# The first head pair's q and k loaded and turned in row halves, with a newly laid out instruction order

## The chip, the cores and the metric

The kernel runs on one NeuronCore of a Trainium2 chip. The metric is the device time of one execution in microseconds (us), here given as the median of several runs. The engines named below are TensorE (PE; its weight loads are listed as PEld), VectorE (DVE), ScalarE (ACT), GpSimd (POOL) and SyncE (SP), which here only issues DMAs.

## The reference

Two layers follow each other. The first is attention with a mixture of blocks: for each of 4 batches x 8 heads, a sequence of 768 positions with head dimension 64 is cut into 12 key blocks of 64. Each query scores the mean key of every block that is not later than its own, keeps the best three and its own block, and attends causally inside those:

```
k_rep = k.reshape(B, H, 12, 64, D).mean(axis=3)
gate  = einsum('bhsd,bhnd->bhsn', q, k_rep)          # later blocks: -1e9
sel   = top3(gate) | {own block};  mask = sel & causal
attn  = softmax(where(mask, q @ k.T / 8, -1e9)) @ v
```

The second takes the heads side by side as x (4 x 768 x 512), mixes it by a two-dimensional Fourier transform, normalizes and applies a two-layer MLP:

```
u   = x + real(fft2(x))                 # over sequence and features
un  = (u - mean) / sqrt(var + 1e-6)
out = u + relu(un @ w1) @ w2            # 512 -> 2048 -> 512
```

## The kernel before, in words

Heads are taken in 16 pairs P (two heads, 128 partitions); four pairs make a batch b. Every step of the kernel is a short token such as `tk:3` (step and pair) or `w:0,5` (step, batch, tile). The text `ORDER` lists all tokens, and each engine executes its instructions strictly in that order. `PLACES` says which buffer each tile gets. Nothing is reordered later, so an engine that waits holds all of its own later instructions.

Steps for a pair P:

- `Lk`, `Lq`, `Lv` (`load`, lines 284 to 309): DMAs issued by SP that bring k, q and v. The first pair's q and k are loaded by `consts_first` (line 755) instead, one k half by ACT's queue.
- `tk`, `tq` (`a_tp`): k and q are turned so that the head dimension lies on partitions. For P of 2 to 6 that is TensorE's transpose, six tiles of 128x128 a tensor (line 350). For the pairs in `R3` it is a matmul with an identity matrix per head and row triple (line 338, 12 instructions a tensor, which the profile lists as 24). From P = 7 on DVE does it (line 325).
- `ks`, `kh` (lines 353 to 366): DVE sums the keys of each block, and the sums are spread over the two heads of the pair (`half`, on POOL).
- `kc`, `qc`, `qs`: k copied to 16 bit by ACT, q copied out of PSUM by DVE (for P = 0 half by ACT, half by DVE), q cast by POOL.
- `g`, `gt`, `gx`, `gl`, `gm`: PE computes the gate scores, DVE turns them, finds the best three, compares and turns the mask back.
- `K` (P of 7 and more): POOL copies the mask into extra rows of q, eight copies of 32x160 (`stage_K`).
- `s`, `e`, `d`: six score tiles a pair on PE, their exponentials on ACT (line 507), the causal cut on the diagonal on POOL (line 513).
- `vc`, `v`, `x`: v cast on POOL, product with v on PE, division on DVE.

Steps for a batch b: `fs`, `fd`, `f`, `fc` fold x for the Fourier transform (DVE, a little POOL); `y`, `ty`, `tr`, `m`, `u`, `nm`, `xu`, `xt`, `un` do the transform and the normalization's mean (PE, ACT, DVE in turn); `w`, `r` are the first MLP product and its ReLU (16 tiles); `bn`, `nv`, `nr` the variance; `c`, `o`, `od` the second MLP product, the sum and the output. `W` and `X` are POOL-issued loads of the MLP's weights.

`iz` spreads a small constant (`indc`, loaded by ACT's queue) over two tiles on ACT; the masks of pairs 0 to 6 need it. Before any of this PE runs nine matmuls of zeros (`warmps`, line 772) while the first loads are on their way.

Of the kernel before, what the change touches and what calls it, by code (L numbers as in the profile page):

```python
# [11 lines left out]
FP = mybir.dt.float32  # L12
# [79 lines left out]
for _pieces in SC_TILES:  # L92
# [16 lines left out]
R3 = (0, 1)  # L109
# [20 lines left out]
d:4,1 d:4,2 d:4,0 d:5,0 Lv:4 d:4,5 vc:4 v:4 xu:0,5 xt:0,4 xt:0,5 un:0,2 nm:0,1,1 xu:0,1 nm:0,2,1  # L130
xt:0,0 xt:0,1 un:0,0 x:4 nm:0,3,1 w:0,5,2 w:0,6,2 xu:0,3 w:0,5,0 xu:0,2 xt:0,2 xt:0,3 w:0,6,0
w:0,4,2 w:0,4,0 un:0,1 w:0,5,1 Lk:7 tk:7 gx:6 gl:6,0 ks:7 gl:6,1 gm:6 d:5,3 qs:7 W:2 kh:7 d:5,1
# [3 lines left out]
w:0,13 r:0,13 Lq:8 tq:8 Lc:0 K:7 s:7,5 e:7,5 s:7,2 e:7,2 w:0,15 r:0,15 d:6,3 d:6,4 d:6,1 d:6,5 kh:8  # L136
s:7,4 g:8 gt:8 gx:8 d:7,5 qs:8 X:0 Lv:6 vc:6 Lk:9 tk:9 gl:8,0 ks:9 Lq:9 tq:9 gl:8,1 fs:5,0 fs:5,1
gm:8 e:7,4 d:7,4 s:7,1 e:7,1 s:7,0 e:7,0 d:7,0 d:7,2 d:6,2 w:0,1 r:0,1 w:0,9 w:0,10 r:0,10 r:0,9
kc:8 bn:0,0 v:6 s:7,3 w:0,12 r:0,12 x:6 bn:0,4 bn:0,3 fs:6,0 fs:4,1 w:0,8 r:0,8 e:7,3 w:0,11 r:0,11
kh:9 X:1 qs:9 K:8 s:8,3 e:8,3 fs:4,0 g:9 gt:9 s:8,1 s:8,0 s:8,4 e:8,0 e:8,1 gx:9 gl:9,0 fs:6,1  # L140
gl:9,1 gm:9 d:7,1 Lv:7 vc:7 d:7,3 v:7 x:7 fd:6,1 fd:6,0 fs:7,1 fs:7,0 fd:7,0 bn:0,2 c:0,0,0 c:0,2,0
c:0,1,0 K:9 d:8,3 kc:9 e:8,4 Li:0 s:9,1 e:9,1 s:9,0 e:9,0 c:0,3,0 fd:7,1 fc:1 f:1,0 f:1,2 f:1,1 nv:0
nr:0 s:9,5 e:9,5 f:1,3 y:1,1,0 y:1,1,1 ty:1,1 tr:1,1 Lv:9 Lk:10 tk:10 ks:10 y:1,0,0 y:1,0,1 ty:1,0
tr:1,0 Lk:11 tk:11 ks:11 s:9,4 e:9,4 c:0,3,1 c:0,2,1 s:8,2 o:0,3 Lq:10 o:0,2 tq:10 Lk:12 m:1,2 u:1,5
e:8,2 kc:10 od:0,3 od:0,2 Lq:11 Lq:12 Lv:8 c:0,1,1 kh:10 g:10 d:8,2 d:9,5 gt:10 gx:10 u:1,4 m:1,0
u:1,0 s:9,3 e:9,3 c:0,0,1 s:8,5 e:8,5 d:9,0 kh:11 vc:9 u:1,1 tk:12 gl:10,0 m:1,1 u:1,3 u:1,2 o:0,1
gl:10,1 gm:10 tq:11 o:0,0 ks:12 nm:1,4,2 nm:1,0,2 xu:1,5 xu:1,4 un:1,4 s:9,2 e:9,2 nm:1,2,2 xu:1,1
un:1,1 c:0,4,0 c:0,4,1 o:0,4 kc:11 xu:1,3 un:1,3 xu:1,0 un:1,0 d:8,0 d:9,4 d:9,3 qs:10 d:8,1 d:9,1
d:9,2 v:9 g:11 K:10 s:10,4 e:10,4 gt:11 x:9 gx:11 gl:11,0 gl:11,1 tq:12 gm:11 c:0,5,0 xu:1,2 un:1,2
s:10,0 s:10,3 s:10,2 e:10,3 e:10,2 bn:1,5 c:0,5,1 o:0,5 bn:1,1 e:10,0 s:10,1 e:10,1 qs:11 d:8,5  # L150
d:8,4 vc:8 v:8 s:10,5 e:10,5 x:8 K:11 s:11,4 e:11,4 fs:9,0 d:10,4 s:11,2 kh:12 g:12 gt:12 e:11,2
s:11,0 s:11,1 e:11,0 e:11,1 s:11,3 e:11,3 d:11,4 d:11,1 d:10,3 d:10,1 d:11,3 d:10,0 un:1,5 w:1,11
r:1,11 fs:9,1 w:1,3 r:1,3 Lk:13 tk:13 gx:12 gl:12,0 gl:12,1 Lv:11 Lq:13 gm:12 K:12 w:1,15 s:11,5
e:11,5 d:11,0 w:1,0 w:1,14 r:1,14 kc:12 w:1,10 bn:1,2 r:1,15 ks:13 kh:13 d:11,5 d:11,2 vc:11 r:1,0
Lk:14 od:0,4 Lv:10 r:1,10 w:1,2 w:1,9 r:1,9 bn:1,4 d:10,5 qs:12 w:1,13 tq:13 r:1,2 Lv:14 bn:1,0 g:13
r:1,13 d:10,2 v:11 vc:10 bn:1,3 Lv:12 nv:1 s:12,5 w:1,12 od:0,5 e:12,5 gt:13 gx:13 Lk:15 w:1,7
r:1,12 x:11 kc:13 w:1,6 gl:13,0 r:1,7 od:0,1 fs:8,0 s:12,4 gl:13,1 Lq:14 gm:13 s:12,3 e:12,4 fs:8,1
v:10 K:13 tk:14 e:12,3 w:1,1 x:10 kc:14 qs:13 w:1,5 tk:15 Lq:15 r:1,1 w:1,4 r:1,5 fs:11,0 ks:15 nr:1
r:1,6 s:13,1 ks:14 od:0,0 s:13,5 w:1,8 e:13,5 r:1,4 fs:10,0 tq:14 s:12,2 r:1,8 fs:11,1 c:1,0,0
fd:11,1 e:13,1 tq:15 kh:15 kh:14 s:13,3 fs:10,1 s:12,1 fd:10,1 c:1,1,0 fd:11,0 e:12,1 fd:10,0 fc:2  # L160
e:13,3 f:2,1 f:2,2 s:13,0 e:12,2 f:2,3 c:1,0,1 f:2,0 e:13,0 d:12,2 d:13,3 s:12,0 d:12,3 g:15 e:12,0
d:12,5 g:14 d:13,1 c:1,1,1 gt:14 vc:14 gx:14 Lv:15 y:2,0,0 o:1,1 y:2,1,0 o:1,0 y:2,1,1 od:1,1
y:2,0,1 ty:2,1 c:1,4,0 vc:15 ty:2,0 tr:2,1 Lv:13 tr:2,0 od:1,0 m:2,1 d:12,1 d:12,0 d:13,0 m:2,0
u:2,3 u:2,2 c:1,4,1 u:2,0 nm:2,2,2 u:2,1 m:2,2 gl:14,0 nm:2,0,2 gl:14,1 xu:2,2 gm:14 bn:2,2 xu:2,3
c:1,5,0 K:14 gt:15 gx:15 c:1,2,0 o:1,4 vc:12 u:2,4 od:1,4 un:2,3 qs:14 gl:15,0 u:2,5 c:1,3,0 bn:2,3
nm:2,4,2 xu:2,5 un:2,2 bn:2,0 xu:2,1 d:13,5 s:13,4 qs:15 c:1,3,1 e:13,4 un:2,1 gl:15,1 bn:2,5 xu:2,4
un:2,5 s:13,2 gm:15 xu:2,0 c:1,2,1 e:13,2 un:2,0 kc:15 d:13,2 d:13,4 s:14,0 un:2,4 o:1,3 d:12,4
# [34 lines left out]
def kernel(  # L202
# [113 lines left out]
    def XW(P):  # L316
        return 1 if P in (0, 1, 2, 6) else 0
# [548 lines left out]
```

## Time and profile before

| | |
|---|---|
| median of 3 runs | 284.73 us (284.0 to 284.99) |
| profiled execution | 284.95 us |
| its span, first to last instruction | 283.3 us |
| busy: PE, DVE, ACT, POOL | 276.4, 188.7, 167.6, 122.3 us |
| granted TensorE clock | 1.00 in the whole span |

The span is what the profiler saw between the first and the last instruction; the 1.65 us to the execution's own time lie outside of it. Busy times of PE are unions of matmul records whose ends are modelled, so a busy PE isn't always a PE at full rate.

### The profile page before, as it was taken

To read this page: it belongs to the slowest core of one execution; us is meant where nothing else is said; L and a number is where in the kernel's file an instruction comes from. 1 tells how busy PE (TensorE), PEld (TensorE's weight loads), DVE (VectorE), ACT (ScalarE), POOL (GpSimd) and SP (SyncE) were. 2 spreads that over 40 slices of the span, in tenths; PEclk is the share of its full clock that TensorE was granted. 3 is DMA by queue.
4 is the path that set the end of the run, shared out by engine and by line. 5 is a ranking of instruction groups with operands and counts; after the bars stand their busy time and mean duration, and the time that the engine had idled before them with its cause. 6 is when DMAs were issued, how large, how long until landed. Compare 5 with 4: busy or idle time off the path is not lost.

```text
span 283.3 us, 6782 instructions
## 1 busy us (share of the span) xinstructions
PE 276.4 (98%) x2629; PEld 172.7 (61%) x2629; DVE 188.7 (67%) x568; ACT 167.6 (59%) x221; POOL 122.3 (43%) x314
## 2 busy tenths in 40 slices
PE   8999999999999999999999999999999999999995
PEld 4756677776566655556665475566575554565454
DVE  1689999998799699978979669550276452380032
ACT  2698989859869456794787634669641261343100
POOL 2164956724896726854946627711522000002000
PEclk9999999999999999999999999999999999999999
DMA  7999999999599959579497062420000042000045
GB/s 200 222 227 208 242 178 172 187 174 164 87 169 197 146 101 184 98 147 153 112 203 134 1 179 74 106 91 0 2 0 2 1 130 59 0 37 2 0 154 180
DMA packets 117040, 33.45 MB, mean 118 GB/s; under 512 B 107600, under 2 KB 113808, under 8 KB 117008
## 3 DMA queue, kind: packets, MB, share of 16 engines
q1 hardware_dynamic: 112928, 28.62, 50.1%
q0 software_dynamic: 3664, 4.19, 9.5%
q8 instruction: 20, 0.33, 0.5%
q10 hardware_dynamic: 416, 0.20, 0.2%
q14 instruction: 12, 0.10, 0.1%
HBM read 28.55 MB, written 6.29 MB: 123 GB/s over the span
## 4 chain that ended last, share of the span: by engine, by line
PE 84%; DVE 9%; POOL 3%; ACT 2%; issue 2%; DVEq 0%; POOLq 0%
PE h L710 30%; PE c L735 25%; PE sc L490 6%; PE av L525 6%; POOL qk L246 2%; PE yp L595 2%; PE sc L485 2%; DVE u L641 2%; PE tp L350 1%; PE g L408 1%; PE warmps L772 1%; PE tp L338 1%; PE mx L627 1%; PE sc L497 1%; PE c L728 1%
## 5 line engine op out<-in xcount | busy, mean ns | idle before, releaser
L507 ACT ACTIVATE pt<-sc 128x1024 f16<-128x1024 f32 (+1 forms) x96 | 83.8, 919 | 26.3 <-PE sc L490 19.4
L710 PE MATMUL h<-unT,w 128*128 128x256 f16 (+1 forms) x528 | 87.5, 321 | 0.0
L735 PE MATMUL c<-w_sb,hT 128*128 128x512 f16 x368 | 83.7, 379 | 0.0
L710 PEld LDWEIGHTS <-w 128*128 128x128 f16 x528 | 50.8, 98 | 31.0 <-issue 0.3
L735 PEld LDWEIGHTS <-hT 128*128 128x128 f16 x368 | 35.7, 98 | 40.7 <-issue 0.3
L720 ACT ACTIVATE hT<-h 128x768 f16<-128x768 f32 x48 | 37.8, 808 | 37.1 <-PE h L710 36.9
L513 POOL TENSOR_SCALAR_AFFINE_SELECT pt<-pt 128x256 f16<-128x256 f16 x96 | 38.3, 420 | 34.7 <-ACT pt L507 34.1
L747 DVE SCALAR_TENSOR_TENSOR u<-c,rs,u 128x512 f32<-128x512 f32 (+2 forms) x26 | 17.6, 701 | 35.1 <-PE c L735 32.1
L246 POOL TENSOR_SCALAR_AFFINE_SELECT qk<-mt 32x160 f16<-32x160 f16 x72 | 23.8, 351 | 19.1 <-DVE mt L462 17.6
L718 DVE TENSOR_SCALAR hT<-h 128x768 f16<-128x768 f32 x16 | 15.2, 952 | 23.7 <-PE h L710 23.5
L490 PE MATMUL sc<-qk 96*128 96x512 f16 (+3 forms) x144 | 27.2, 306 | 0.1
L525 PEld LDWEIGHTS <-pt 128*128 128x128 f16 x672 | 22.1, 97 | 2.7 <-POOL pt L513 1.0
L525 PE MATMUL av<-v,pt 128*128 128x65 f16 x672 | 23.0, 193 | 0.3 <-POOL pt L513 0.3
L246 POOL TENSOR_SCALAR_AFFINE_SELECT qk<-q 64x768 f16<-64x768 f32 (+1 forms) x25 | 21.1, 844 | 4.3 <-DVE q L386 3.3
L243 POOL TENSOR_TENSOR t<-vr,rs 128x6 f32<-128x6 f32 x12 | 2.8, 235 | 40.5 <-DVE rs L686 39.8
L490 PEld LDWEIGHTS <-qk 96*128 96x128 f16 x144 | 13.1, 98 | 8.9 <-issue 1.4
L641 DVE SCALAR_TENSOR_TENSOR u<-mx,x 128x512 f32<-128x512 f32 x24 | 15.4, 685 | 1.9 <-PE mx L628 1.8
L655 ACT ACTIVATE x<-u,nm 128x512 f16<-128x512 f32 x24 | 16.3, 715 | 0.3
L246 POOL TENSOR_SCALAR_AFFINE_SELECT v<-nat 128x768 f16<-128x768 f32 x16 | 14.6, 915 | 4.1 <-DMA nat<-in_v_dram 3.9
L675 DVE BATCH_NORM_STATS2 bst<-u 128x6 f32<-128x512 f32 x24 | 16.1, 671 | 0.0
L243 DVE TENSOR_TENSOR x<-av,rcp 128x768 f16<-128x768 f32 x16 | 15.3, 957 | 0.6
L485 PE MATMUL sc<-qk 64*128 64x512 f16 (+3 forms) x112 | 14.6, 306 | 0.8 <-DVE q L386 0.5
(105 smaller groups left out, 323.2 us busy)
## 6 DMA issues: line engine op xcount, KB each, us to landing
nat<-in_v_dram SPq DMA_DIRECT2D x16, 384.0 KB, 4.9
out_dram<-u SPq DMA_DIRECT2D x23, 256.0 KB, 2.4
nat<-in_q_dram SPq DMA_DIRECT2D x36, 96.0 KB, 3.7
nat<-in_k_dram SPq DMA_DIRECT2D x36, 96.0 KB, 3.5
nat<-in_q_dram SPq DMA_DIRECT2D x14, 192.0 KB, 4.6
nat<-in_k_dram SPq DMA_DIRECT2D x13, 192.0 KB, 4.9
w_sb<-in_moe_w_ch_dram POOLq DMA_DIRECT2D x2, 1024.0 KB, 11.9
w<-in_moe_w_ch_dram POOLq DMA_DIRECT2D x2, 768.0 KB, 7.6
```

Of the source, the lines that this page charges most:

```text
L243: (eng or nc.vector).tensor_tensor(out=out, in0=in0, in1=in1, op=op)
L246: nc.gpsimd.affine_select(out=out, in_=in_, pattern=[[0, i] for i in n], base=0, channel_multiplier=0, compare_op=ALU.is_ge, fill=0.0)
L485: nc.tensor.matmul(ps[:, e, co:co + q1 - q0], qk[hs[e], 1, XW(P), 128 * jt:128 * jt + 128], qk[hs[e], 0, XW(P), q0:q1], start=(co == 0), s ...
L490: nc.tensor.matmul(ps[:, e, co:co + q1 - q0], qk[0:96, e, 1, 128 * jt:128 * jt + 128], qk[0:96, e, 0, q0:q1], start=True, stop=True)
L507: nc.scalar.activation(out=d["pt"][:, o:o + 2 * n].rearrange("p (e c) -> p e c", e=2), in_=d["sc", i][:, :, 0:n], func=AF.Exp, scale=0.125)
L513: nc.gpsimd.affine_select(out=dg, in_=dg, pattern=[[0, 2], [1, 128]], base=0, channel_multiplier=-1, compare_op=ALU.is_ge, fill=0.0)
L525: nc.tensor.matmul(av[:, e, 66 * st:66 * st + 65], pt[:, co:co + 128], vv[:, e, jt, 0:65], start=(cnt == 0), stop=(cnt == 20))
L641: nc.vector.scalar_tensor_tensor(out=u_t[b, kp][:, k2, :].rearrange("p (m two) -> p two m", two=2), in0=mps[:, k2, :].rearrange("p (two m) ...
L710: nc.tensor.matmul(hp[:, l:r], w1s, unT[:, dt, l:r], start=(dt == 0), stop=(dt == NDT - 1))
L720: nc.scalar.activation(out=hT, in_=hp, func=AF.Relu)
L735: nc.tensor.matmul(c_ps[b, g[0]][:, st - g[0], :], h_t[b, it][:, 128 * st:128 * (st + 1)], w2_t[0][:, it, :], start=(it == 0), stop=(it == ...
L747: nc.vector.scalar_tensor_tensor(out=o, in0=ps, scalar=st_t[b][1][:, st:st + 1], in1=o, op0=ALU.mult, op1=ALU.add)
```

## The change

The first pair's q and k are no longer loaded as 768-byte runs per head and partition with both heads in one DMA, and no longer turned by the `R3` matmuls. Each tensor is cut into two halves of 384 rows. Each half has three consecutive rows per partition as before, but the two heads are put side by side, so each row arrives as a piece of 256 bytes; head 0 is issued by SP and head 1 by ACT. A half is turned by three 128x128 transposes, which write every third column of a PSUM tile of their own. Key sums, the k copy and the q copy run per half, and `kh:0` moves from POOL to DVE. `R3` keeps pair 1 alone. The order and the places are new up to `bn:1,0 g:13`; from there on the order is the old one, token for token.

```diff
-R3 = (0, 1)
+R3 = (1,)
```
```diff
 def a_tp(P, who, h=None):
...
+        if P == 0:
+            d["tp", who, h] = ps = pst([128, S // 2], f"tp{who}{h}_0")
+            for st in range(3):
+                nc.tensor.transpose(ps[:, st:S // 2:3], src[:, 3 * h + st, :], id32)
             return
```
```diff
 def a_sums(P, h=None):
+        if P == 0:
...
+            nc.vector.tensor_reduce(out=pairs[P]["kr12"][:, NB // 2 * h:NB // 2 * (h + 1)],
+                                    in_=pairs[P]["tp", 1, h].rearrange("p (n c) -> p n c", c=64),
+                                    axis=mybir.AxisListType.X, op=ALU.add)
+            return
 def a_half(P):
...
-           nc.gpsimd)
+           nc.gpsimd if P else nc.vector)
 def a_k(P, h=None):
+        if P == 0:
+            nc.scalar.copy(out=qk[:, 1, XW(P), S // 2 * h:S // 2 * (h + 1)], in_=pairs[P]["tp", 1, h])
+            return
 def a_q32(P, h=None):
+        if P == 0:
...
+            (nc.vector.tensor_copy if h else nc.scalar.copy)(
+                out=pairs[P]["q32"][:, S // 2 * h:S // 2 * (h + 1)], in_=pairs[P]["tp", 0, h])
+            return
```
```diff
 def consts_first():
-            t = apool.tile([128, 2, 2, 192], ...)
-            for h, eng in ((0, nc.sync), (1, nc.scalar)):
-                (nc.sync if who == 0 else eng).dma_start(t[:, h], rows3(src, 0, 0, h))
+            t = apool.tile([128, NST, 2, 64], ...)
+            for h in range(2):
+                for e, eng in ((0, nc.sync), (1, nc.scalar)):
+                    eng.dma_start(t[:, 3 * h:3 * h + 3, e, :], src[0, e, S // 2 * h:S // 2 * (h + 1)]
+                                  .rearrange("(p r) d -> p r d", r=3))
```

The beginning of the order:

```diff
-tk:0 Lk:1 kc:0 ks:0 kh:0 tq:0 qc:0 qs:0 tk:1 kc:1 iz:0 iz:1 g:0 gt:0 gx:0 gl:0,0 gl:0,1 gm:0 Lk:2
-tk:2 Lq:1 tq:1 qc:1 kc:2 s:0,4 e:0,4 s:0,3 s:0,2 ks:1 qs:1 kh:1 Lv:0 ks:2 e:0,3 g:1 gt:1 gx:1 gl:1,0
...
+tq:0,0 qc:0,0 Lk:1 tk:0,0 ks:0,0 tk:0,1 ks:0,1 kc:0,1 tq:0,1 kh:0 kc:0,0 qc:0,1 qs:0 tk:1 ks:1 kh:1
+g:0 gt:0 gx:0 gl:0,0 gl:0,1 gm:0 Lk:2 tk:2 Lq:1 tq:1 qc:1 qs:1 ks:2 kh:2 iz:0 iz:1 s:0,2 kc:1 e:0,2
+s:0,5 e:0,5 g:1 gt:1 gx:1 gl:1,0 gl:1,1 gm:1 kc:2 s:0,4 e:0,4 s:0,3 s:0,0 e:0,0 e:0,3 Lq:3 Lq:2 tq:2
...
```

Around batch 0's Fourier stage, up to the first MLP tile:

```diff
-s:3,5 s:4,3 e:3,5 e:4,3 s:4,2 e:4,2 d:3,1 d:3,5 v:3 x:3 fs:3,1 fs:3,0 fd:2,1 fd:3,0 fd:3,1 s:5,1
-e:5,1 W:1 Lq:6 Lk:6 LF:0 LT:0 s:5,3 e:5,3 s:4,4 e:4,4 d:4,4 s:4,0 tq:6 qc:6 s:4,1 e:4,1 s:5,2 e:5,2
-e:4,0 tk:6 kc:6 fc:0 f:0,0 f:0,1 y:0,0,0 y:0,0,1 ty:0,0 f:0,2 y:0,1,0 f:0,3 y:0,1,1 Lq:7 tq:7 ks:6
-s:5,5 e:5,5 s:5,0 ty:0,1 tr:0,0 tr:0,1 e:5,0 s:4,5 s:5,4 e:5,4 m:0,0 u:0,0 u:0,1 e:4,5 nm:0,0,1
-xu:0,0 m:0,2 u:0,4 nm:0,4,1 xu:0,4 u:0,5 nm:0,5,1 qs:6 d:4,3 W:0 kh:6 m:0,1 g:6 gt:6 u:0,3 u:0,2
...
-xt:0,0 xt:0,1 un:0,0 x:4 nm:0,3,1 w:0,5,2 w:0,6,2 xu:0,3 w:0,5,0 xu:0,2 xt:0,2 xt:0,3 w:0,6,0
...
+v:2 gl:5,1 x:2 fs:2,0 fs:2,1 gm:5 fs:1,1 fd:2,1 fd:2,0 s:3,1 e:3,1 d:3,1 W:1 s:4,1 e:4,1 s:4,2 s:4,3
+e:4,3 e:4,2 v:3 x:3 fs:3,1 fs:3,0 fd:3,1 fd:3,0 f:0,1 fc:0 f:0,0 s:4,5 s:5,2 e:5,2 e:4,5 d:4,5 s:4,0
+e:4,0 d:4,0 s:5,0 e:5,0 LT:0 Lq:6 Lk:6 s:5,1 tk:6 ks:6 e:5,1 d:4,2 d:5,2 d:4,3 s:4,4 e:4,4 d:5,1
+y:0,0,0 y:0,0,1 ty:0,0 kc:6 f:0,2 f:0,3 y:0,1,0 y:0,1,1 ty:0,1 tr:0,0 tr:0,1 s:5,3 e:5,3 s:5,4 e:5,4
+LF:0 m:0,0 u:0,0 nm:0,0,1 xu:0,0 u:0,1 nm:0,1,1 m:0,2 s:5,5 e:5,5 u:0,4 nm:0,4,1 xu:0,1 u:0,5
+nm:0,5,1 m:0,1 u:0,2 u:0,3 xt:0,0 tq:6 qc:6 xt:0,1 un:0,0 W:0 Lv:4 vc:4 d:4,1 kh:6 d:4,4 d:5,0 v:4
+xu:0,4 xt:0,4 nm:0,2,1 xu:0,5 xt:0,5 un:0,2 g:6 gt:6 xu:0,2 nm:0,3,1 xu:0,3 xt:0,2 xt:0,3 w:0,6,2
...
```

The stretches between the gate and the first score tile of pairs 7 and 10:

```diff
-r:0,5 w:0,6,1 r:0,6 w:0,7,2 w:0,4,1 w:0,7,0 r:0,4 w:0,7,1 r:0,7 s:6,0 e:6,0 s:6,2 e:6,2 g:7 gt:7
-bn:0,1 bn:0,5 Lk:8 tk:8 gx:7 ks:8 gl:7,0 gl:7,1 gm:7 d:5,2 d:5,5 d:5,4 d:6,0 w:0,2 s:6,5 e:6,5 r:0,2
-s:6,4 e:6,4 s:6,3 e:6,3 s:6,1 e:6,1 w:0,3 w:0,0 r:0,0 r:0,3 Lv:5 vc:5 kc:7 w:0,14 r:0,14 v:5 x:5
-w:0,13 r:0,13 Lq:8 tq:8 Lc:0 K:7 s:7,5 e:7,5 s:7,2 e:7,2 ...
+r:0,7 w:0,13 d:5,4 W:2 ... qs:7 s:6,5 e:6,5 Lv:5 s:6,0 kh:7 g:7 gt:7 gx:7
+gl:7,0 gl:7,1 gm:7 e:6,0 bn:0,1 Lq:8 Lc:0 tq:8 Lq:9 w:0,14 r:0,14 r:0,13 w:0,15 w:0,12 r:0,15 kh:8
+vc:5 v:5 x:5 K:7 d:6,2 qs:8 kc:7 r:0,12 s:7,2 e:7,2 ...
...
-e:8,2 kc:10 od:0,3 od:0,2 Lq:11 Lq:12 Lv:8 c:0,1,1 kh:10 g:10 d:8,2 d:9,5 gt:10 gx:10 u:1,4 m:1,0
...
-d:9,2 v:9 g:11 K:10 s:10,4 e:10,4 ...
+u:1,2 s:9,3 e:9,3 u:1,3 nm:1,2,2 m:1,0 g:10 gt:10 gx:10 g:11 qs:11 d:9,2 d:9,4 d:9,3 c:0,4,0 gl:10,0
+gl:10,1 gm:10 nm:1,4,2 xu:1,4 xu:1,2 kc:10 un:1,4 u:1,0 u:1,1 nm:1,0,2 xu:1,1 un:1,1 v:9 x:9 gt:11
+c:0,4,1 o:0,4 gx:11 gl:11,0 gl:11,1 xu:1,0 un:1,0 xu:1,5 K:10 s:10,4 e:10,4 ...
```

The launch code, all other functions and the work done are the same.

More of the change, by code (lines that the diff above doesn't have):

```diff
@@ L138 @@
[L138 to L143, printed above, removed]
@@ L317, in XW, with a_tp @@
         return 1 if P in (0, 1, 2, 6) else 0
-    def a_tp(P, who):
+    def a_tp(P, who, h=None):
         d = pairs[P]
@@ L329, in a_tp @@
             src = nat[P, who].rearrange("p h e (r d) -> p h e r d", r=3)
[L330 to L334 removed]
+            d["tp", who] = ps = pst([128, 2, 512], f"tp{who}_{P}")
+            to = [ps[:, h, 0:S // 2] for h in range(2)]
             for h in range(2):
```

150 lines of the change are left out of this document (73 added, 77 removed).

## The prediction

> **What bounds the kernel now.** I read the page's slices and chain first, then busy time by stretches, then the chain in order of time up to the first MLP matmul. The page:
>
> ```profile
> PE   8999999999999999999999999999999999999995
> ...
> PE 84%; DVE 9%; POOL 3%; ACT 2%; issue 2%; DVEq 0%; POOLq 0%
> ```
>
> PE is on the chain for most of the span. Three stretches (length, then busy time of PE, PEld, DVE, ACT, POOL, granted clock, DMA share, GB/s) show where it is alone there:
>
> ```profile
> 15.00:20.00 5.00, 4.69 (x64) 2.75 (x63) 4.42 (x18) 4.66 (x6) 2.50 (x7) 1.00 1.30 229
> 20.00:25.00 5.00, 5.00 (x66) 3.09 (x60) 4.49 (x18) 4.54 (x6) 3.48 (x8) 1.00 1.33 222
> ...
> 200.00:220.00 20.00, 20.00 (x196) 12.93 (x194) 12.12 (x26) 7.53 (x10) 6.48 (x23) 1.00 0.01 2
> ```
>
> From 200 on PE has no gap and the others have room. In the early stretches DVE and ACT are some 90% busy as well, and PE has holes. So the kernel has two stages: up to the first MLP matmul three engines pull together, and behind it PE alone sets the end. The change can move the end by the start of the second stage, and by PE work taken away. The chain in order of time (start, length):
>
> ```profile
> 1.30 4.02 PE warmps L772 x9
> 5.32 2.42 PE tp L338 x24
> 7.74 0.66 PE tp0a L338 x12
> 8.39 0.66 PE tp0b L338 x12
> 9.05 1.31 PE tp L338 x24
> 10.36 0.67 PE g L408 x8
> 11.05 0.49 DVE gt L422
> ...
> 12.92 0.48 DVE mt L462
> ...
> 16.32 0.49 DVE gt L422
> ...
> 20.80 0.81 PE tp L350 x6
> ...
> 51.11 1.93 DVE u L641 x6
> ...
> 56.17 1.41 PE h L710 x12
> 57.57 0.45 PE xt L663 x8
> 58.02 3.93 PE h L710 x36
> ```
>
> The first k (`tk:0`) takes 101 ns an entry, its like 0.66/12 = 55 ns right behind it, and the zero matmuls (512 columns) 447 ns: until about 7.2 PE runs at half rate, though the clock is shown as 1.00. The first mask (`mt`) is ready at 13.40, the second gate's turn starts at 16.32, the first MLP matmul at 56.17.
>
> Single instructions that the steps need, from the timeline of the engines:
>
> ```profile
> 0.81 0.48 ACTq L761 DMA_DIRECT2D nat<-in_k_dram  x1
> 1.34 0.96 SPq L761 DMA_DIRECT2D nat<-in_q_dram  x2
> 1.32 1.28 ACT L768 ACT_TABLE_LOAD   x1 [1.32 <-PEq L850]
> 8.62 0.96 DVE L359 TENSOR_REDUCE kr<-tp 128x12 f32<-128x768 f32 x1 [6.13 <-ACT qk L370]
> 9.50 0.55 DVE L384 COPY q<-tp0b 128x384 f32<-128x384 f32 x1
> 13.85 5.28 ACT L507 ACTIVATE pt<-sc 128x1024 f16<-128x1024 f32 x6 [0.49 <-PE sc L497]
> 43.86 0.95 DVE L389 COPY q<-tp 128x768 f32<-128x768 f32 x1
> 47.23 0.96 DVE L325 STREAM_TRANSPOSE q<-nat 128x768 f32<-128x768 f32 x1
> 46.71 0.82 ACT L373 CAST qk<-tp 128x768 f16<-128x768 f32 x1
> 47.39 1.08 ACT L608 CAST ty<-yp 128x772 f16<-128x772 f32 x1
> 48.53 0.38 ACT L507 ACTIVATE pt<-sc 128x256 f16<-128x256 f32 x1
> 52.07 0.72 ACT L655 ACTIVATE x<-u,nm 128x512 f16<-128x512 f32 x1
> 55.93 1.34 ACT L655 ACTIVATE x<-u,nm 128x512 f16<-128x512 f32 x2
> ```
>
> **Step 1, the loads: nothing.** q and k of pair 0 are 4 x 196.6 KB. The DMA view of the first 14 us, in 40 slices of 0.35 us, and the landing of ACT's load:
>
> ```profile
> GB/s 0 0 0 0 0 53 108 257 345 369 364 342 268 156 244 274 299 315 301 295 228 159 202 328 301 290 219 271 283 241 227 217 246 190 244 175 168 261 154 68
> nat<-in_k_dram ACTq DMA_DIRECT2D x1, 192.0 KB, 3.4
> ```
>
> In long runs they move at 345 to 369 GB/s, and the slices add up to 786 KB at about 4.9 us. The 1024 runs become 3072 pieces. For such pieces I take 229 GB/s, the row 15 to 20 us, where SP's q, k and v loads all come in 256-byte pieces. From 146 KB at 2.8 us, the first q half, third in the queue, is complete at 2.8 + 444/229 = 4.75 and everything at 5.6. ACT's load is told as landed at 0.81 + 3.4 = 4.2, some 0.7 behind the point where the slices have both k halves, so I add 0.7: 5.45 and 6.3. PE wants the first q half at 5.32, when the zero matmuls end, and the second at 7.5, so the cost is 0.1, which I round to nothing. The zeros hide it; were they shorter, every tenth that they end earlier would be lost in waiting. At the slowest slice of that time, 159 GB/s, the first q half costs 1.0: that is the upper bound. Below nothing it can't go, as PE is busy until 5.32. SP issues four DMAs instead of three ahead of `Lk:1` (0.5 later), and ACT four (0.48 each) ahead of its 1.28 table load, which then ends at 4.1; ACT's next work waits for the zeros' end anyway. k of pair 1 (long runs, 290 GB/s by the slices from 4.9 on) lands at 5.6 + 1.36 + 0.7 = 7.65 and is wanted at 7.9.
>
> The Trainium skill ("DMA: Bandwidth & Descriptors", Specifications) states that a transfer needs 512 B or more for line rate, which speaks against this change. The rows agree in kind (229 against 345 to 369); by the rule alone the sum would lose the same 0 to 1.0.
>
> **Step 2, turning pair 0 on PE: 1.16 us less.** Before: 2.42 + 0.66 + 0.66 = 3.74, to 9.05. After: 12 transposes of 128x128, at 0.81/6 = 0.135 (row of L350) at full rate and twice that before 7.2. That is 7 by 7.2 (1.88/0.27) and 5 x 0.135 behind it: PE is through at 7.89, and with `tk:1` (1.31) at 9.2. The gate `g:0` then ends at 9.87 instead of 11.03. At full rate the work taken off PE is 48 x 0.055 - 12 x 0.135 = 1.0.
>
> **Step 3, the first masks on DVE: 0.75 earlier, with more done.** Two half sums (0.48 each, half of 0.96) run at 7.1 and 7.6; `kh:0`, which no row shows on DVE, lies between nothing and another 0.48; the q half (0.55) ends by 9.15. None holds `g:0`, since PE is in `tk:1` until 9.2. But `ks:1` (0.94) now stands ahead of `gt:0` on DVE: 9.2 + 0.94 and a tenth or so for hand-overs, 10.3, instead of 11.05, so the first mask comes at 12.65. Behind it there is one sum less to do: q copy (0.95), `ks:2` (0.94), and `gt:1` at 14.5 instead of 16.32.
>
> **Step 4, from there to the MLP: 0.9 earlier in effect.** I went through both orders and noted which entries stand ahead of each point. DVE has two fewer ahead of `u:0,0`: `qc:6` (0.95) and `tq:7` (0.96). With step 3 it could be 3.7 us earlier. ACT can't: its first exponential comes 0.75 earlier with the mask; up to `ty:0,0` it has `kc:2`, `e:4,5`, `e:5,0` more and `e:5,3`, `kc:6` less, +0.38. So `ty:0,0` starts at 47.39 - 0.75 + 0.38 = 47.0 if ACT's waits stay. Then 3.8 us of ACT work follow without a hole (1.08, `kc:6` 0.82, two exponentials) and the first `xu` starts at 50.8 instead of 52.07. The new order puts all six `xu` and `e:5,5` (0.38) ahead of the first MLP matmul: from 52.07 to 57.27 were 5.2, now 5.6, and with one turn the MLP starts at 56.6. In the old order 1.41 us of MLP stood before the last turns at 58.02, so the two are level (58.02 - 1.41 = 56.61); what stays of step 2 on PE is then lost in waiting, and the end moves by 0.1 at most.
>
> That is with ACT's waits of the first stage unchanged:
>
> ```profile
> ACT pt L507 <- PE sc L497: 2.2, 5, 0.9
> ```
>
> This is the row for 5 to 56 us; with 0.49 ahead of the first exponential, about 1.7 are left, all for scores that wait for a mask. Masks come 0.75 to 1.85 earlier and DVE has less to do, so they could go, but ACT's entries were also dealt out anew. I take half, 0.8: the MLP starts at 55.8.
>
> **Sum.** -0.1 - 0.8 = -0.9 us. The profiled execution of 284.95 (span 283.3 and 1.65 around it) would be 284.05; the median of the runs shown is 0.22 below it, so the time is 284.73 - 0.9 = 283.8. The end itself (the order from `g:13` on, the output) is untouched. A measurement of this kernel can tell about 0.3% (0.85 us) from no change.
>
> **Rivals.** (a) *PE runs dry between gate and scores.* In the new order the work that PE has between `g:7` and the first score of pair 7, and between `g:10` and that of pair 10, shrinks. Rows:
>
> ```profile
> 82.49 2.69 POOL L246 TENSOR_SCALAR_AFFINE_SELECT qk<-mt 32x160 f16<-32x160 f16 x8
> ...
> 105.04 1.73 PE c L735 x8
> 106.76 0.45 PE g L415 x8
> ...
> 113.65 0.36 DVE mt L462
> ...
> 70.09 1.28 PE av L525 x42
> ```
>
> For pair 10 it was `g` 0.45, `g:11`, four halves of the second product (1.73), three of the transform and more: 10.0; it will be 2 x 0.45 + 2 x 1.73 + 1.28 = 5.6. For pair 7: 0.45 + 3 x 3.93/3 + 1.28 = 5.7 instead of 10. In that time DVE must make the mask (2.35 for pair 0, from 11.05 to 13.40, with nothing between) and POOL the eight copies (2.69): 0.45 + 2.35 + 2.69 = 5.5. In the old trace pair 10's mask took from 107.2 to 114.0, because DVE had other work. From 0.1 (pair 10) and 0.2 (pair 7) on, each tenth by which DVE or POOL are behind at these places is lost on PE. At 1.3 behind it is 1.2 + 1.1 = 2.3: 283.8 + 2.3 = 286.1. For it: these two engines are the ones that the new order loads more heavily early. Against: there is no old hole on PE behind 60. (b) *ACT's waits all go*: the other 0.9 as well, which DVE's lead allows: 282.9, and 282.4 if half of the 1.0 of PE work from step 2 also shows. (c) *ACT's waits stay*: 284.6, no measurable change. (d) *The clock is released one step later.* Before, PE was on real matmuls when it went to full rate at 7.2; now it is on transposes there. If these don't count, half rate lasts longer; the one interval that the trace shows is 5.9, from the zeros' start to full rate, so it is at most to 13.1, and I price half of it, to 10.15. 12 transposes at 0.27 end at 8.56, `tk:1` (15 entries at 0.107, 9 at 0.055) at 10.65, and `gt:0` stands at 11.7: 1.4 later than in step 3, so 283.8 + 1.4 = 285.2. Against it: nothing in the trace, as all transposes there come later at full rate. The Trainium skill ("TensorE: Matmul & The Clock Gate", Part 4) states that full clock doesn't engage for transpose mode; no row here shows it either way. (e) *The pieces of 256 B are slower than I take them* (159 GB/s): q's first half costs 1.0 and `tk:1` waits as long, 284.8: the change would not bring forward what it says.
>
> **How the numbers follow.** Forecast 0.33, of which 0.30 is past 0.3%; (b) 0.12; (a) 0.31; (c) 0.13; (d) 0.05; (e) 0.06. Faster: 0.30 + 0.12 = 0.42. Slower: (a), 0.31. Same: 0.03 + 0.13 + 0.05 + 0.06 = 0.27. (d) and (e) lie under 0.3%. The range goes from the far end of (b), 282.3, to just beyond the price of (a), 286.2, which leaves out its tail and little below. The forecast's own range is 283.0 to 284.4.
>
> **What would show it.** Right: the first transposes start at 5.3 and end by 7.9 with the rate changing near 7.2; `g:0` near 9.2; the first mask at 12.6; first `xu` before 51; PE full from 56 to the end. Wrong: a PE wait ahead of pair 7's or 10's scores with POOL as releaser (a); transposes at 0.27 beyond 7.5 (d); PE idle behind the zeros (e); the first exponential before 13.2 but the first MLP matmul behind 56.6 (c).

## The result, and the profile after

| | before | after |
|---|---|---|
| median | 284.82 us (22 executions, 283.78 to 286.22) | 285.31 us (22 executions, 284.31 to 286.2) |
| profiled execution | 284.95 us (span 283.3) | 284.31 us (span 282.6) |

The ratio is 1.0025, with an interval of 1.0013 to 1.0037: the change costs a quarter of a per cent (the ratio goes by all executions and is not the quotient of the two medians, which lie 0.49 apart). The forecast was 283.8, a gain of 0.9; the range 282.3 to 286.2 holds the result.

The two profiled executions say the opposite, 0.64 us faster. The profile after is the fastest of its 22 executions, while the one before is near the middle of its own. So the profile after shows what the change does at its best, and even there it doesn't win: the fastest execution of before took 283.78.

The page's slices and chain of waits, after:

```profile
PE   6899998999999999999999999999999999999995
...
PE 82%; DVE 7%; POOL 3%; ACT 3%; issue 2%; DMA 1%; SPq 1%; POOLq 0%; DVEq 0%
```

The first slice of PE has fallen from 8 to 6, and two things that the chain of before didn't have are on it: a DMA and its issue by SP. Busy time by stretches, after (columns as in the prediction):

```profile
15.00:20.00 5.00, 4.70 (x76) 3.29 (x74) 3.92 (x19) 5.00 (x7) 1.94 (x3) 1.00 1.08 205
20.00:25.00 5.00, 5.00 (x90) 4.10 (x84) 4.81 (x17) 4.80 (x6) 3.56 (x11) 1.00 1.15 227
200.00:220.00 20.00, 20.00 (x197) 13.13 (x196) 11.55 (x25) 7.66 (x10) 6.48 (x23) 1.00 0.01 2
```

From 15 to 25 PE still shares the work with DVE and ACT, and from 200 on it is alone, as before. The chain in order of time (start, length), after:

```profile
0.81 0.71 SPq L771
...
1.58 0.82 SPq L771
...
2.44 3.73 DMA nat<-in_q_dram
...
6.31 1.50 PE tp L342 x12
...
7.82 1.54 PE tp L335 x24
...
9.38 0.96 DVE kr L362
10.34 0.40 DVE gt L431
...
12.11 0.48 DVE mt L471
...
55.53 3.92 PE h L719 x32
```

It no longer begins with the zero matmuls but with SP's issues and the load of the first q half. PE's own timeline has the gap (in brackets: idle time ahead, and what ended it):

```profile
1.30 4.02 PE L783 MATMUL warmps<-zeros 128*128 128x512 f16 x9 [1.30 <-DVE half L784]
6.31 1.50 PE L342 MATMUL tp<-id,nat 128*128 128x128 f32 x12 [0.99 <-DMA nat<-in_q_dram]
7.82 1.53 PE L335 MATMUL tp<-id,nat 128*64 128x128 f32 x24
```

The zeros end at 5.32 and PE stands for 0.99 us. Then twelve transposes take 1.50, 0.125 each, all at full rate, and are through at 7.81: within 0.1 of the predicted 7.89. That is luck, as they began 0.99 late and none of them ran at half rate, where the prediction had no wait and seven at half rate. The gate, the masks and the first MLP matmul also come within 0.3 of the prediction. So its times fit this one execution, and yet the median went the other way. The experiments search for the reason.

### The profile page after: what moved, and what is told of

Its sections match the earlier page's. It is cut to its first block, busy times and chain, and to the rows that moved or that the text cites. A ratio compares the mean times of both kernels' runs of the same rounds, so it can differ in the third digit from the quotient of the medians.

```text
span 282.6 us, 6718 instructions
## 1 busy us (share of the span) xinstructions
PE 273.6 (97%) x2593; PEld 170.0 (60%) x2593; DVE 189.2 (67%) x570; ACT 166.3 (59%) x222; POOL 120.5 (43%) x313
## 4 chain that ended last, share of the span: by engine, by line
PE 82%; DVE 7%; POOL 3%; ACT 3%; issue 2%; DMA 1%; SPq 1%; POOLq 0%; DVEq 0%
PE c L744 28%; PE h L719 28%; PE sc L499 7%; PE av L534 6%; PE yp L604 3%; ACT pt L516 2%; PE mx L636 2%; PE mx L637 2%; DVE kr L362 1%; DMA nat<-in_q_dram 1%; PE c L737 1%; PE g L424 1%; POOL qk L246 1%; DVE mx L447 1%; PE sc L494 1%
## 5 line engine op out<-in xcount | busy, mean ns | idle before, releaser
L516 ACT ACTIVATE pt<-sc 128x1024 f16<-128x1024 f32 (+1 forms) x96 | 82.8, 925 | 24.6 <-PE sc L499 17.5
L617 ACT CAST ty<-yp 128x772 f16<-128x772 f32 x7 | 7.2, 1036 | 14.4 <-PE yp L604 14.4
```

The lines of the kernel that those rows point to most:

```text
L516: nc.scalar.activation(out=d["pt"][:, o:o + 2 * n].rearrange("p (e c) -> p e c", e=2), in_=d["sc", i][:, :, 0:n], func=AF.Exp, scale=0.125)
```

## The experiments

Names used in the expectations: theories S and L put the loss on the late pieces, M on the middle of the new order, H on the moment at which PE goes to full rate (it depends on the hole behind the zeros), T on the transposes (they do not count for the clock), the other letters are explained where they stand. "Late" and "early" are executions in which PE goes to full rate late or early. A "hole" is idle time of PE between the zero matmuls and its first real work. Ratios are to the kernel before, run beside the experiment: a median of 284.77 in experiments 1 to 4.

**1. The changed kernel again**, no edit.

> The changed kernel once more. Theory S (the start): how late the first q pieces land behind the zero matmuls differs between executions and moves the whole kernel; the first profile (284.31, the fastest of 22) had a wait of 1.0 us there. So this profile, if it is of a slower execution, shows a longer wait at the first transposes and the same distances behind it: 284.3 plus the extra wait. Theory M (the middle): the spread comes from the new order between 15 and 125 us, where loads and masks are tighter; then the first transposes start at 6.3 again and a gap on PE of 0.5 to 2 us stands later. Theory N: median about 285.3 and no single place.

Measured: 285.7 (12 executions), ratio 1.0025 [1.0005, 1.0045]. Its profiled execution took 285.87. PE's timeline:

```profile
6.13 2.79 PE L342 MATMUL tp<-id,nat 128*128 128x128 f32 x12 [0.81 <-DMA nat<-in_q_dram]
```

The wait is no longer than in the profile after (0.81 against 0.99); so the length of the wait is not what differs between executions, against what theory S expected. What differs is the rate: the same twelve transposes take 2.79, 0.23 each, and the 24 entries of `tk:1` behind them, from 8.93 on, 2.03 instead of 1.54. At 107 ns instead of 55 an entry, this is nine or ten entries at half rate, up to about 9.9. The trace files also hold records of the granted clock which the page and its views don't print for the start. The first one of this run stands at 10.01, that of the profile after at 5.42, and that of the profile before at 7.26. The first gate's turn starts at 11.86 instead of 10.26, and the execution ends 1.56 later. The 34 executions of the changed kernel in the two runs fall in two groups, 11 at 284.31 to 284.99 and 23 at 285.21 to 286.2.

**2. The old order** with the new loads and transposes:

```diff
-tq:0,0 qc:0,0 Lk:1 tk:0,0 ks:0,0 tk:0,1 ks:0,1 kc:0,1 tq:0,1 kh:0 kc:0,0 qc:0,1 qs:0 tk:1 ks:1 kh:1
+tk:0,0 tk:0,1 Lk:1 kc:0,0 kc:0,1 ks:0,0 ks:0,1 kh:0 tq:0,0 tq:0,1 qc:0,0 qc:0,1 qs:0 tk:1 kc:1 ...
```

> The new loads and transposes of pair 0, but the old order behind them (k turned first, places renamed to fit). Theory S: the cost of the late pieces stays; k lands before q, so PE waits some tenths and the 12 short transposes give back about 1.2: level with before within 0.5, 284.3 to 285.3. Theory M (the order is what costs): the new order's loss is gone and the shorter turn remains, about 0.9 faster than before, 283.9.

Measured: 284.89, all twelve within 284.66 to 285.02; ratio 0.9997 [0.9977, 1.0018]. PE's timeline:

```profile
1.30 3.68 PE L782 MATMUL warmps<-zeros 128*128 128x512 f16 x9 [1.30 <-DVE half L783]
4.81 0.49 PE L341 MATMUL tp<-id,nat 128*128 128x128 f32 x3
5.58 0.52 PE L341 MATMUL tp<-id,nat 128*128 128x128 f32 x3 [0.28 <-DMA nat<-in_k_dram]
6.33 0.52 PE L341 MATMUL tp<-id,nat 128*128 128x128 f32 x3 [0.23 <-DMA nat<-in_q_dram]
7.14 0.52 PE L341 MATMUL tp<-id,nat 128*128 128x128 f32 x3 [0.29 <-DMA nat<-in_q_dram]
```

Here the zeros are at full rate before they end (3.68 instead of 4.02), so the early start of PE is as good as it can be. The transposes are still not through before 7.66, as each group of three waits for its half: the loads set the pace, and the last half is there at 7.1 only. The gate's turn starts at 9.94, 1.1 ahead of the profile before, yet the time is the same. Beside a second profile of before, with full rate at 5.2 and the turn at 10.09 (experiment 11), the lead is 0.15, and at 19.96 a gate's turn starts 0.5 later than there. In between PE waits twice for k loads that are queued behind the pieces, which the second profile of before doesn't:

```profile
10.15 0.85 PE L345 MATMUL tp<-id,nat 128*128 128x128 f32 x6 [0.28 <-DMA nat<-in_k_dram]
...
17.91 0.85 PE L345 MATMUL tp<-id,nat 128*128 128x128 f32 x6 [0.52 <-DMA nat<-in_k_dram]
```

So the old order gives the lead back at its later loads. The time lies where theory S had it.

**3. Long runs with identity matmuls, in the new order**: halves as 768-byte runs, turned as the kernel before does it, half by half.

```diff
-                nc.tensor.transpose(ps[:, st:S // 2:3], src[:, 3 * h + st, :], id32)
+                for e in range(2):
+                    nc.tensor.matmul(ps[64 * e:64 * e + 64].rearrange("p (i r) -> p r i", r=3)[:, r, :],
+                                     src[:, h, e, r, :], id32, start=True, stop=True)
...
-            for h in range(2):
-                for e, eng in ((0, nc.sync), (1, nc.scalar)):
+            for h, eng in ((0, nc.sync), (1, nc.scalar)):
+                eng.dma_start(t[:, h], rows3(src, 0, 0, h))
```

> The new order, but pair 0's q and k come in 768-byte runs as before and each half is turned by six identity matmuls. Theory S: no wait at 5.3, but 48 entries of turning instead of 12 transposes: first gate near 10.2 instead of 9.28, so about 0.9 later than the changed kernel's good executions, 285.2, with the small spread of before. Theory M: the spread of the changed kernel stays and the median is 0.9 above it, 286.2.

Measured: 284.63 (284.05 to 285.86), ratio 1.0008 [0.9985, 1.003]; its profile is of 284.05. PE's timeline:

```profile
5.24 2.84 PE L343 MATMUL tp<-id,nat 128*64 128x128 f32 x48
7.91 1.48 PE L335 MATMUL tp<-id,nat 128*64 128x128 f32 x24
```

No wait, but 48 entries: through at 8.0 instead of 7.81, and the gate's turn starts at 10.31 instead of 10.26. The transposes save as much as their loads cost in waiting. The median lies under both theories: S asked for 285.2 and M for 286.2.

**4. k ahead of q** in the changed kernel's order, as its loads come:

```diff
-tq:0,0 qc:0,0 Lk:1 tk:0,0 ks:0,0 tk:0,1 ks:0,1 kc:0,1 tq:0,1 kh:0 kc:0,0 qc:0,1 qs:0 tk:1 ks:1 kh:1
+Lk:1 tk:0,0 ks:0,0 kc:0,0 tk:0,1 ks:0,1 kc:0,1 tq:0,0 qc:0,0 tq:0,1 kh:0 qc:0,1 qs:0 tk:1 ks:1 kh:1
```

> The changed kernel with both k halves turned ahead of q, in the order in which they are loaded. Theory S: PE starts when the first k half is there (5.3 to 5.6 instead of 6.3) and is through at about 7.1 instead of 7.8; the spread from q's landing shrinks: 0.7 faster than the changed kernel, 284.6. Theory M: no change from the changed kernel beyond 0.2, 285.3.

Measured: 285.32 (284.71 to 285.73), ratio 1.0018 [0.9997, 1.0038]. PE's timeline up to 11 us, and the one wait from 20 to 24:

```profile
5.11 2.04 PE L342 MATMUL tp<-id,nat 128*128 128x128 f32 x9
7.41 0.52 PE L342 MATMUL tp<-id,nat 128*128 128x128 f32 x3 [0.25 <-DMA nat<-in_q_dram]
...
21.69 0.85 PE L346 MATMUL tp<-id,nat 128*128 128x128 f32 x6 [0.15 <-DMA nat<-in_k_dram]
```

The hole of 0.99 is gone, and the first gate's turn starts at 10.39, no earlier: the last q half is what PE waits for. Nine transposes ran at 0.22 and the full rate came at about 7.0 (the first clock record stands at 6.94), when PE had run nothing but transposes for 1.8. At 21.7 the k of pair 3 is late, and by 26 everything is 0.9 later (the turn of pair 3's gate at 26.86 instead of 25.94): a second way in which the same start can end later. The median is the one that theory M gave; the loss in this profile stands at a load.

**5. Twelve zero matmuls** instead of nine in the changed kernel, which bridges the hole; **6. identity matmuls** on the changed kernel's loads, which keeps the hole and takes the transposes away; **7. five zeros** in the kernel before. The edits:

```diff
-        for _ in range(9):
+        for _ in range(12):     # and range(5) in the kernel before
```
```diff
-                nc.tensor.transpose(ps[:, st:S // 2:3], src[:, 3 * h + st, :], id32)
+                for e in range(2):
+                    nc.tensor.matmul(ps[64 * e:64 * e + 64, st:S // 2:3],
+                                     src[:, 3 * h + st, 64 * e:64 * e + 64], id32, start=True, stop=True)
```

> The changed kernel with 12 zero matmuls instead of 9, so that TensorE is busy from 1.3 us until the first q half has landed (6.1 to 6.2) and the hole of 0.8 to 1.0 us behind the zeros is gone; nothing else differs. Theory H (the hole): the moment at which PE goes to full rate differs from execution to execution, and it comes late (about 10 us) where the hole breaks the busy stretch; without the hole it comes between 4.6 and 8.1. Then the executions at 285.2 to 286.2 vanish, all lie between 284.3 and 285.1, median about 284.6, 0.7 under the changed kernel; in the profile the twelve transposes are through before 8.6. Theory T (transposes do not count as work for the clock): the late executions stay, the median is 285.3 or above, and where the zeros end at half rate the transposes take 0.23 each. Theory O (the order, not the start, makes the loss): median 285.3, with spread as before.

> The changed kernel (256-byte pieces, hole behind the zeros), but the halves of pair 0 are turned by 48 identity matmuls, as the kernel before does it, instead of 12 transposes. Theory T: the clock now counts them, the late executions go; at full rate the 48 take 2.64 instead of 1.5, so the end is at about 285.3 in all executions with little spread (284.9 to 285.7). Theory H: the hole stays and so do the late executions, now later by the added work: the early ones at 285.0 to 285.6, the late ones at 286.3 to 287.3 (48 at 0.107 up to about 10.4), median about 286.3.

> The kernel before with 5 zero matmuls instead of 9: they end at 3.54, and k (landed about 4.2) leaves a hole of some 0.7 us, on a kernel with long runs, identity matmuls and the old order. Theory H: a hole at this place delays the release here too: the turning of pair 0 stays at 0.1 an entry up to 9 or 10, and although it starts 1.1 earlier, the time is not better; median 284.8 to 285.6. Theory T: the hole does nothing, pair 0 is turned 1.1 earlier at most, of which the old order keeps 0.2 to 0.5: 284.3 to 284.6.

Measured beside 284.46 for the kernel before: twelve zeros 285.06, ratio 1.0014 [0.9998, 1.0031]; identity matmuls 285.36, 1.0041 [1.0021, 1.0061]; five zeros 284.43, 1.0009 [0.9987, 1.0032].

Twelve zeros: five executions at 284.19 to 284.32 and seven at 285.01 to 285.42. The upper group is as frequent as in the changed kernel, so theory H fell in its strong form, but it is lower: it ends at 285.42 instead of 286.2. Theory T, by which slow transposes last to 9.4, asks for 286 and more, and no execution was there.

Identity matmuls: nine of twelve at 284.98 to 285.58, three at 286.08 to 287.44. Of these the one at 286.08 has a span like the nine (283.5, they up to 283.8), so two are late. The median is the one that theory T gave, the late executions are those of theory H. Its profile (286.96) shows a late one without a single transpose of pair 0:

```profile
6.17 4.56 PE L343 MATMUL tp<-id,nat 128*64 128x128 f32 x48 [0.85 <-DMA nat<-in_q_dram]
```

95 ns an entry up to 10.7; the first clock record stands at 9.74. A hole of 0.85 with real matmuls behind it can put off the full rate to about 10 by itself, so this doesn't need the transposes.

Five zeros in the kernel before: its real work starts at 3.89 after a wait of 0.28. The times spread to 283.36 below and 287.04 above, and the median stayed, as theory T had it (284.3 to 284.6); H asked for 284.8 or more.

**8. and 9. Fewer zeros without a hole**: seven in the kernel before, eight in the kernel of experiment 3. **10. and 11. A second profile** of twelve zeros and of the kernel before.

> The kernel before with 7 zero matmuls instead of 9: at half rate they end at 4.43, behind k's landing (4.05 in the profile with 5 zeros), so there is no hole, and the real work starts 0.9 earlier. So far the time follows the start of the first gate's turn on DVE (gt) plus 274.0 +- 0.2 in seven of nine profiles, in the old order as in the new. Theory H (release late where PE has a hole, otherwise between 4.6 and 8.1): no execution with a late release, all earlier by 0.4 to 0.9: median 283.8 beside 284.6 for the kernel before, ratio 0.997, and none above 285. Rival W (the zeros decide when full rate comes, hole or not: less heating, later release): median 284.4 or above, with late executions at 285 to 287 as with 5 zeros.

> The new order with long runs and identity matmuls (the kernel that took 284.63 against 284.77) with 8 zero matmuls instead of 9: they end at 4.88 at half rate, about when the first q half lands. Theory H: no hole, 0.45 earlier: median 284.2, ratio to the kernel before 0.999; early executions at 283.7. Rival W: median 284.6 or above.

> The changed kernel with 12 zeros again, for a second profile. Its times fell in two groups, 284.19 to 284.32 and 285.01 to 285.42, and the profile was of the early one. If this look falls in the late group: theory H: the zeros take 5.3 or so (half rate to their end at 6.66), and PE goes to full rate while the transposes run, at 7.5 to 8.4, so their row takes 2.0 to 2.4; the first gate's turn starts 1.0 later than 10.20. Theory T (no release on transposes): they all take 0.23, 2.8 in all, up to 9.4, and the gate's turn starts at 12 or later, for a time of 286 or more, which the twelve times speak against.

> The kernel before again, for a second profile. Its times reach from 283.57 to 286.2 while its first profile (284.95, full rate from 7.2) is a late one. If this look is an early one (under 284.2): the zeros end at about 5.0 or earlier, pair 0's 48 entries take 2.6 to 2.8, and the first gate's turn starts at 9.6 to 10.2, ahead of the changed kernel's best (10.20 to 10.26). Whatever it is, the time is that start plus 274.0 +- 0.2.

Seven zeros: 284.29 beside 284.92, ratio 0.9979 [0.9958, 1.0], the lowest median of all; the expected 283.8 was not reached. None was above 285.07, so rival W, which had late executions up to 287, fell here. Its profile is of the slowest of its executions (285.07). The gate's turn starts there at 9.43, 1.6 ahead of the profile before, and the lead is lost on the way, when DVE waits for the q of pair 7, a load of the old order:

```profile
47.32 0.98 DVE L325 STREAM_TRANSPOSE q<-nat 128x768 f32<-128x768 f32 x1 [1.19 <-DMA nat<-in_q_dram]
```

Eight zeros with long runs: 284.97 beside 284.92, ratio 1.0002 [0.9979, 1.0026]; PE waited 0.34 for the first q half and started at 5.21, as with nine. Nothing was won, since the load was next. Theory H missed (284.2); the median is one that rival W allows, and no profile fell on an execution of its upper half.

The second profile of twelve zeros fell on the lower group again (284.31): the zeros at half rate to 6.6, the twelve transposes in 1.56. What PE does in an execution of the upper group without a hole was therefore not shown.

The second profile of the kernel before settles most. It took 284.03, and PE was at full rate when the real work began:

```profile
5.25 1.53 PE L338 MATMUL tp<-id,nat 128*64 128x128 f32 x24
6.61 0.82 PE L338 MATMUL tp0a<-id,nat 128*64 128x128 f32 x12
7.26 0.82 PE L338 MATMUL tp0b<-id,nat 128*64 128x128 f32 x12
7.92 1.48 PE L338 MATMUL tp<-id,nat 128*64 128x128 f32 x24
```

Pair 0 is turned by 7.92 here, instead of 9.05 in the profile on which the prediction rests, and by 7.81 in the profile after. The last product of the MLP, from the chain of each (before, its second profile, after, then the changed kernel again):

```profile
278.49 1.80 PE c L728 x32
```

```profile
277.54 1.80 PE c L728 x32
```

```profile
277.57 1.80 PE c L737 x32
```

```profile
279.13 1.80 PE c L737 x32
```

With the full rate there at the start of the real work in both, the change moves the end of PE's work by 0.03 us: it brings nothing there. And yet the span is 282.3 in the second profile of before and 282.6 after. The difference is behind PE: from the landing of the last output to the end of the span it takes 1.04 there and 1.29 after. In the trace files SP ends with eight waits for outstanding transfers, one after another. The last landing releases the sixth of them there and the second after, and each wait left over takes 0.06. All eight profiles with 256-byte pieces have this longer end (1.27 to 1.29), with either order and with identity matmuls too; the six with long runs don't (1.03 to 1.04). So in every profile the change costs 0.25 here, whatever its start.

**12. The loads in the order in which they are turned**: first q half, both k halves, second q half.

```diff
-        for who in (1, 0):
...
-            for h in range(2):
+        for who, h in ((0, 0), (1, 0), (1, 1), (0, 1)):
```

> The changed kernel, but the eight loads of pair 0 are issued in the order in which the halves are turned: first q half, both k halves, second q half (the changed kernel issues both k halves first, and turns the first q half first). Theory L (what the change loses is the wait for this half, 0.8 to 1.0 on PE, as much as the transposes save): the half now lands near 5.0, the hole behind the zeros is 0.2 or less, and the turning is through by 6.9 in an early execution. Next late is the k of pair 1, issued at 3.81 and landed near 7.7, so an early execution gains only 0.1 (284.1 to 284.3), but a late one 0.5 to 1.0, as its slow transposes run in what was the hole: median 284.6 to 284.8, upper end 285.4 instead of 286.2, ratio to the kernel before 1.000. Rival T (the spread of the changed kernel comes from the transposes, which delay the full rate, not from the hole): the late executions stay at 285.2 to 286.2 and the median above 285.1, although the hole is gone.

Measured: 285.1 (284.13 to 285.46), ratio 1.0013 [0.9995, 1.0031]. PE's timeline:

```profile
5.11 0.97 PE L342 MATMUL tp<-id,nat 128*128 128x128 f32 x6
6.23 0.52 PE L342 MATMUL tp<-id,nat 128*128 128x128 f32 x3 [0.16 <-DMA nat<-in_k_dram]
7.25 0.52 PE L342 MATMUL tp<-id,nat 128*128 128x128 f32 x3 [0.49 <-DMA nat<-in_q_dram]
7.87 1.53 PE L335 MATMUL tp<-id,nat 128*64 128x128 f32 x24
```

The hole is gone, but the last half lands near 7.1, not by 6.3, and the turning is through at 7.77 and not at 6.9. The early executions therefore gained nothing, and the upper end fell to 285.46, as with twelve zeros. Eight of twelve are at 284.97 and above. Theory L holds for the upper end and for what bounds the early executions, and missed the median; the upper group stays here as well.

The profiles of this case side by side (full rate: first clock record in the trace file, with which the lengths of the zeros', pair 0's and `tk:1`'s rows agree; turn: start of the first gate's turn on DVE):

| kernel | hole behind the zeros | full rate from | turn | time | time less turn |
|---|---|---|---|---|---|
| before | none | 7.26 | 11.05 | 284.95 | 273.90 |
| before, second profile | none | 5.23 | 10.09 | 284.03 | 273.94 |
| after | 0.99 | 5.42 | 10.26 | 284.31 | 274.05 |
| after, again | 0.81 | 10.01 | 11.86 | 285.87 | 274.01 |
| long runs | none | 5.16 | 10.31 | 284.05 | 273.74 |
| twelve zeros | 0.43 | 5.02 | 10.20 | 284.20 | 274.00 |
| identity matmuls | 0.85 | 9.74 | 12.95 | 286.96 | 274.01 |
| five zeros, before | 0.28 | 5.77 | 9.62 | 283.80 | 274.18 |
| q half first | none | 5.36 | 10.31 | 284.34 | 274.03 |

The time is the first gate's turn plus 274.0, within 0.3, in the old order and in the new; experiments 9 and 10 fit too (274.10 and 273.86). The exceptions are experiments 2 (275.05), 4 (274.97) and 8 (275.64), all three with a load that came late further on. The column hides terms that cancel: the new order with long runs has 0.2 less than before, and the pieces add the 0.25 at the end.

## Why the prediction was wrong

**What failed: carrying the sum to the median.** Between the two profiles the sum held: the last product starts at 277.57 instead of 278.49, 0.92 earlier, and 0.9 was forecast. But it was made against a profile with the full rate from 7.2, and this moment was taken as a property of the kernel ("half rate before 7.2"). It is a property of the execution: in the four profiles of the two kernels, all with nine zeros, it came at 5.2, 7.3, 5.4 and 10.0. So the 0.92 is the difference between a late execution of before (3.74 for the turning) and an early one of the changed kernel, and taking it off the median of before was the wrong step. Step 2 forecast 1.16, and its end fell 1.24 earlier (9.05 and 7.81), by the luck told above. Where both have the full rate at the start, the turning ends at 7.92 and 7.81: 0.1 is left, as the hole takes the rest.

**Step 1, the loads, was mis-sized.** "Nothing" was a wait of 0.8 to 1.0, the upper bound that the text gave; the first q half landed at 6.17 and not at 5.45. Two terms were short. A load of 256-byte pieces keeps SP for 0.71 and 0.82 instead of 0.46, so the first q half, third in SP's queue, is issued at 2.44, where lengths like those of before give 1.8. And it took 3.73 from there. The last half landed near 7.1, not 6.3 (experiment 12), and in each order tried the turning was through at 7.66 to 7.93 (experiments 2, 4 and 12). The rate of 229 GB/s was a small part of the error, as the DMA view of the first 14 us after, in slices of 0.35, shows:

```profile
GB/s 0 0 0 0 0 0 93 201 263 181 148 158 256 285 260 165 193 261 324 355 259 248 249 237 253 253 272 314 309 284 263 245 222 225 219 213 215 222 258 206
```

From 2.8 to 5.95 the mean is 212, which makes 0.15 over the 444 KB up to the first q half. The hole is worth what the twelve transposes save over the 48 entries (2.64 at 55 ns, less 1.50): 1.1 won, 1.0 lost. The rule named there (the Trainium skill, "DMA: Bandwidth & Descriptors", Specifications: 512 B or more for line rate) spoke against the change, and the trace agrees in sign, with the 0.99.

**The end was not untouched.** The prediction left the output as it was. It costs 0.25 more (experiment 11), so the span after is 0.65 shorter than in the profile before, and not 0.9.

**Steps 3 and 4 held in place, 4 in part by compensation.** First mask ready at 12.59 (predicted 12.65), second gate's turn 14.55 (14.5), first MLP matmul 55.53 (55.8). ACT's waits for scores from 5 to 56:

```profile
ACT pt L516 <- PE sc L506: 2.7, 4, 1.3
```

1.27 of it stands ahead of the first exponential, which leaves 1.4, against 1.7 before: 0.3 went, not 0.8. But this row is a part of ACT's idle time. All of it, from the first exponential to `ty:0,0`, fell from 2.6 to 1.65, and ACT's work there shrank by 0.3 where 0.38 more was forecast; then ACT waits 1.18 for `u:0,0`. Against the second profile of before, the new order wins 0.3 between the first gate's turn (0.17 later) and the MLP (55.53 against 55.19 and 0.45 for the turns that follow there). It gives 0.3 back once behind 56:

```profile
84.22 1.44 PE L534 MATMUL av<-v,pt 128*128 128x65 f16 x42 [0.30 <-POOL v L246]
```

**The rivals.** (a), PE dry between gate and scores of pairs 7 and 10, fell: this v cast is the only wait of PE that the view of waits lists from 56 on. (b), all of ACT's waits gone, fell too. (c) was right that most of ACT's waits for scores stay, but put the loss there. (e) named the wait behind the zeros and priced it at 1.0, which is the measured size, though not through a rate of 159 GB/s; it had 0.06. (d), a later full rate, had 0.05 and 285.2, close to the median. Late executions exist as it described them, but not for its reason. In experiment 4 the full rate came at 7.0 with nine transposes run since 5.1, and in experiment 6 it came late without transposes. The Trainium skill ("TensorE: Matmul & The Clock Gate", Part 4) has it that transposes don't engage the full clock; experiment 4 speaks against that. Part 1 of the same page of the Trainium skill says that the clock is released after a busy window of some 3.4 us that runs freely, whatever the kernel does. PE is busy from 1.3, so an estimate by that rule has the release between 4.7 and 8.1 where PE has no hole, and one or two windows later where a window holds the hole. The clock records agree but for 0.2: 4.5 to 7.3 without a hole or with a short one (the 4.5 in experiments 2 and 8), about 10 in two of three profiles with 0.8 and more.

**What stays open.** The median is 0.49 above before. The longer end, in every profile with pieces, makes 0.25 of it. The hole accounts for the height of the upper group, whose top falls from 286.2 to 285.4 when it is bridged (experiment 5) or gone (12). Whether the median falls with it isn't settled: the medians there are still 0.6 and 0.46 above before, with ratios of 1.0014 and 1.0013, whose intervals overlap that of the change. The group's share was 23 of 34 with the hole, 7 and 8 of 12 without, and no profile fell on such an execution without a hole. The times of before hold something else as well: beside the experiments, 42 of its 104 executions have 1.8 to 2.9 us outside of the span, while the 34 of the changed kernel have 1.65 to 1.77, and no profile shows what it is. Experiment 3's execution at 285.86 is of this kind (span 283.4). By the span alone the medians beside experiment 1 are 282.7 for before and 283.95 for the changed kernel, so the change itself costs more than the times tell. So it is shown where the expected gain went; why more of the changed kernel's executions lie high is shown in part.

## What to carry to other kernels

Before a saving at the start of a kernel is counted, look at more than one execution: the moment at which PE reaches full rate moved the start by more than the change did, and the difference of two single profiles, one late and one early, looked like a saving of the change. A faster turn of the first tile is worth nothing beyond the landing of its load; smaller pieces cost twice, in the length of the issue and in the landing, and every load queued behind moves too. When several profiles are at hand, look for the one event whose start plus a constant gives the time: here it told in one column that the rest of the order, taken as a whole, was not the cause. It doesn't show terms that cancel, so compare the stretch behind the last product as well.

## What the runs showed of the hardware

- The moment of full rate on PE, with the first matmul always at 1.30, ranged from 4.5 to 10.0 us. The page and its views give the granted clock as 1.00 all along, before and after; the first clock record in the trace file and the lengths of the rows show the moment (zeros 447 ns each at half rate, transposes 0.23 against 0.125).
- A transpose of 128x128 in fp32 takes 0.125 at full rate, as much as 2.3 identity matmuls of 128x64 (55 ns), each of which turns half as much.
- A DMA of 96 KB in 256-byte pieces kept SP for 0.62 to 0.82, one of 192 KB in 768-byte runs for 0.46.
- From the last landing to the end of the span it took 1.03 to 1.04 us in the six profiles with long-run loads and 1.27 to 1.29 in the eight with pieces: the waits that SP still has in its row behind that landing take 0.06 each.
